# One attention, expert and gated-MLP kernel: routing weights transposed before they are normalised, and block outputs spread over steps

## The chip, the cores and the metric

The kernel runs as one program on one core of a Trainium2 chip. A core has a matrix engine (PE), a vector engine (DVE), a scalar engine (ACT), GpSimd (POOL) and a queue engine (SP) that issues most of the DMAs. Each engine works through its own instructions in order, and they meet through semaphores. The metric is the device time of one execution in microseconds; a kernel's time is the median over its runs. A profiled execution, whose time is given as well, has a trace of each instruction.

## The reference, cut to what matters

```python
def _attn_ref(q, k, v, p):                 # 4 batches, 8 heads, 576 tokens, head size 64
    p_packed = sm_attn(p, k, v)            # 32 packed queries
    return sm_attn(q, p_packed, p_packed)

def _moe_ref(x, domain_probs, w1, w2):     # x: 2304 x 512, E = 4 experts, F = 1024
    p = domain_probs / (domain_probs.sum(-1, keepdims=True) + 1e-09)
    for e in range(E):
        h = np.maximum(x @ w1[e], 0.0)
        out += p[:, e:e + 1] * (h @ w2[e])

def _moe2_ref(x, w_in, w_out, s, b):       # 512 -> 2048 -> 512
    r = np.maximum(x @ w_in, 0.0)
    return ((s * (r * r) + b) @ w_out).astype(np.float32)
```

The three run one after the other: attention, then a mixture of four experts in which every token goes through every expert with a weight p, then a gated MLP.

## The kernel before, in words

All large products are made of split operands, a high part (`hh`, `w2h`) and a remainder (`hl`, `w2l`), with three matmuls each.

**Steps of the expert stage.** The main loop runs over 256 steps, one for each (expert e, batch bi, half hf, block f of 128 hidden units). A part is the eight steps (f = 0 to 7) of one (e, bi, hf). In a step, `run(i)` first does what a table `weave` has for that step (attention work for the next batch, weight loads and splits, preparations of the last stage); `advance()` then calls `m1` for a unit two steps ahead, and `m2` works on the step's own unit. `m1` multiplies into a PSUM bank `h` (two of them) and evacuates it with a relu: ACT writes the high part, DVE the remainder. `m2` multiplies that into the accumulators `acc` (four banks, one for each block of 128 tokens). A batch of 576 tokens is four and a half blocks, so that in every second part `m1` leaves 64 columns over, which `rest` keeps, and which `m2` takes up in the part behind it. So 128 of the 256 `m1` calls evacuate two slices of one bank. At the last step of a part, `m2_out` takes each finished block (two or three of them) out of its bank on DVE, scaled by the block's weight from `p_tok`: L771 for e = 0, L774 otherwise, and for e = 3 a transpose L778 into `xt` behind it.

**Deferred work.** When three transposed blocks of a tile of `xt` are there, `x_turn` copies them on ACT into `x2` (L795), which the last stage reads. These copies, in eight pieces for each tile, lie in the list `later`; `go_on()` issues one piece of each list in it per step, behind `m2`.

**The weights p.** `probs` is loaded as 18 rows of 512 numbers (`p_rows`). At step 3 `expert_weights` sums, inverts and multiplies on DVE over 18 partitions (L1004 to L1008), PE transposes the product (L1014, four matmuls), and ACT copies it into `p_tok` (128 tokens x 72). The first use is at the end of the first part.

**What else stands there.** Ahead of the loop, PE has matmuls on zeros (`warm`, L979) in the gaps of the attention of batch 0. At step 3 batch 1's first scores `s` (L200) are computed from `kT`, which DVE transposes (L161). DVE has the maxima (L212) and ACT the copies (L214) of these scores, and the second half of the scores takes the same two banks. POOL makes `w2l` (L597) and parts of batch 0's last softmax (L348, L362). The last stage starts in the last ten steps: `m3` (L893) multiplies `xs` (L837, L838, from `x2`) with `wop`; a gate (L847, L850, L857, L861) gives `gg`, and `m4` (L929) multiplies that with `wo`.

The order within each engine is the order of the calls in the program; no scheduler moves anything.

## Time and profile before

| | |
|---|---|
| median of 3 runs | 1112.1 us (1112.06 to 1112.81) |
| the profiled execution | 1110.32 us |
| its span, first to last instruction | 1108.5 us |
| PE / DVE / ACT / POOL busy | 97% / 63% / 42% / 18% |
| PE idle, waits by line, the 15 largest groups | about 26 us in all, 7.0 of them at one place |
| mean granted clock of PE | 0.994 |

Busy shares say which engine the time goes through; where an engine that is 97% busy still waits, the list of waits gives the line, the engine that it waits for and how long. A granted clock of 1.00 is 2.4 GHz and 0.50 is 1.2 GHz. In a list of waits the columns are the waiting engine and line, the engine and line that ended the wait, and then the total, the number of waits and the longest. In a timeline they are start, duration, engine, line, operation, output and inputs with shapes, and in brackets the idle time before it and what ended it. Where neighbours are merged, x16 says how many a row holds.

### The profile page before, as it was taken

What the parts mean: (1) busy time and instruction counts of PE and PEld (TensorE: products, weight loads), DVE (VectorE), ACT (ScalarE), POOL (GpSimd) and SP (SyncE); (2) the same over time, 40 slices, a digit from 0 to 9 for tenths busy, and PEclk for the clock granted to TensorE, in tenths of its full rate; (3) what the DMA queues carried; (4) which work ended last, traced back from release to release, by engine and by line L of the source; (5) the groups of instructions that cost most, each with busy time, mean ns of one, the idle gap of its engine ahead of it and who ended that gap; (6) DMA issues with size and microseconds to landing.
All of it is one profiled execution on the core that took longest, in us unless ns stands there. A gap on an engine that the chain in (4) does not pass through costs nothing.

```text
span 1108.5 us, 16823 instructions
## 1 busy us (share of the span) xinstructions
PE 1078.5 (97%) x6248; PEld 918.5 (83%) x6248; DVE 694.3 (63%) x1309; ACT 467.7 (42%) x1023; POOL 198.4 (18%) x200
## 2 busy tenths in 40 slices
PE   8799999999999999999999999979999999999998
PEld 5577778878887788888887888869888988989987
DVE  7776665567576446556466644579845766675555
ACT  3433234454344344334435755686532332342121
POOL 1530303131200041001121122144211120210000
PEclk9899999999999999999999999999999999999999
DMA  9640411033116584674675341336756565555532
GB/s 269 194 108 25 104 49 39 10 102 117 57 61 240 194 228 136 202 233 146 220 195 156 102 124 57 124 142 247 281 203 211 181 219 177 210 199 184 196 114 86
DMA packets 66011, 170.21 MB, mean 154 GB/s; under 512 B 10489, under 2 KB 27129, under 8 KB 65931
## 3 DMA queue, kind: packets, MB, share of 16 engines
q1 hardware_dynamic: 65083, 168.03, 47.2%
q10 hardware_dynamic: 848, 1.11, 0.3%
q8 instruction: 50, 0.82, 0.3%
q14 instruction: 30, 0.25, 0.1%
HBM read 122.72 MB, written 46.40 MB: 153 GB/s over the span
## 4 chain that ended last, share of the span: by engine, by line
PE 83%; DVE 8%; ACT 5%; issue 2%; DMA 2%; SPq 1%; POOL 0%; ACTq 0%; DVEq 0%
PE acc L755 28%; PE o L929 18%; PE h L717 16%; PE h L893 15%; ACT x L795 1%; PE pp L518 1%; DVE hl L739 1%; PE s L318 1%; DVE xt L778 1%; DMA v<-in_v_dram 1%; ACT hh L738 1%; DVE acc L774 1%; PE pp L564 1%; PE s L200 1%; PE pv L266 1%
## 5 line engine op out<-in xcount | busy, mean ns | idle before, releaser
L717 PEld LDWEIGHTS h<-a,w1p 128*128 128x128 f32 x1536 | 226.3, 189 | 42.5 <-issue 13.5
L717 PE MATMUL h<-a,w1p 128*128 128x320 f32 (+1 forms) x1536 | 252.2, 299 | 7.5 <-DVE hl L739 4.5
L929 PE MATMUL o<-wo,gg 128*128 128x512 f32 x864 | 225.1, 394 | 2.2 <-DVE gg L861 2.2
L893 PE MATMUL h<-xs,wop 128*128 128x384 f32 x1008 | 206.2, 341 | 4.2 <-DVE xt L778 3.2
L755 PE MATMUL acc<-w2h,hh 128*128 128x512 f32 x512 | 201.9, 394 | 0.0
L755 PE MATMUL acc<-w2l,hh 128*128 128x512 f32 x512 | 201.7, 394 | 0.0
L755 PE MATMUL acc<-w2h,hl 128*128 128x512 f32 x512 | 200.2, 391 | 0.0
L893 PEld LDWEIGHTS h<-xs,wop 128*128 128x128 f32 x1008 | 183.4, 190 | 18.7 <-DVE xt L778 3.5
L739 DVE SCALAR_TENSOR_TENSOR hl<-h,hh 128x256 fp32r<-128x256 f32 x256 | 107.6, 420 | 142.3 <-ACT hh L738 141.7
L929 PEld LDWEIGHTS o<-wo,gg 128*128 128x128 f32 x864 | 160.7, 188 | 27.6 <-DVE gg L861 2.7
L738 ACT ACTIVATE hh<-h 128x256 fp32r<-128x256 f32 x256 | 97.0, 380 | 109.6 <-PE h L717 107.4
L755 PEld LDWEIGHTS acc<-w2h,hl 128*128 128x128 f32 x512 | 96.2, 188 | 22.1
L755 PEld LDWEIGHTS acc<-w2l,hh 128*128 128x128 f32 x512 | 96.4, 188 | 11.9
L755 PEld LDWEIGHTS acc<-w2h,hh 128*128 128x128 f32 x512 | 96.4, 188 | 10.8
L847 ACT ACTIVATE yy<-yy 128x768 f32<-128x768 f32 x48 | 40.3, 839 | 110.7 <-DVE yy L913 110.7
L913 DVE TENSOR_TENSOR yy<-h,uv 128x384 f32<-128x384 f32 x96 | 51.0, 551 | 48.5 <-PE h L893 48.3
L738 ACT ACTIVATE rest<-h 128x64 fp32r<-128x64 f32 x128 | 28.7, 225 | 89.9 <-DVE hl L739 89.9
L795 ACT ACTIVATE x<-xt 32x384 f32<-32x384 f32 x96 | 50.2, 523 | 20.5 <-DVE xt L778 18.9
L857 ACT ACTIVATE gg<-yy,b_sb 128x768 fp32r<-128x768 f32 x48 | 44.9, 935 | 32.0 <-DVE yy L850 31.7
L597 POOL TENSOR_TENSOR w2l<-w2r,w2h 128x512 fp32r<-128x512 f32 x24 | 31.1, 1297 | 129.0 <-ACT w2h L594 104.7
L861 DVE SCALAR_TENSOR_TENSOR gg<-yy,b_sb,gg 128x768 fp32r<-128x768 f32 x48 | 53.2, 1109 | 1.3 <-ACT gg L857 1.3
L739 DVE SCALAR_TENSOR_TENSOR rest<-h,rest 128x64 fp32r<-128x64 f32 x128 | 28.8, 225 | 37.2 <-ACT rest L738 37.2
(387 smaller groups left out, 1171.8 us busy)
## 6 DMA issues: line engine op xcount, KB each, us to landing
xs<-xs_dram SPq DMA_DIRECT2D x63, 768.0 KB, 4.3
w1p_dram<-w1o SPq DMA_DIRECT2D x32, 512.0 KB, 3.8
w1p<-w1p_dram SPq DMA_DIRECT2D x128, 128.0 KB, 4.4
xs_dram<-xs SPq DMA_DIRECT2D x21, 768.0 KB, 3.3
w1r<-in_moe_w_dram SPq DMA_DIRECT2D x12, 512.0 KB, 5.1
w2r<-in_moe_w_dram SPq DMA_DIRECT2D x24, 256.0 KB, 4.1
q<-in_q_dram SPq DMA_DIRECT2D x16, 288.0 KB, 7.0
out_dram<-o_sb SPq DMA_DIRECT2D x17, 256.0 KB, 2.1
```

Of the source, the lines that this page charges most:

```text
L597: nc.gpsimd.tensor_tensor(out=lo, in0=raw_t.pop((e, f)), in1=f32(hi), op=ALU.subtract)
L717: nc.tensor.matmul(t[:, : width(bi, hf)], lhsT=w1p_block(e, bi, f, gi, w), rhs=a2[bi][:, x, gi, part(bi, hf)], start=(n == 0), stop=(n == ...
L738: nc.scalar.activation(hi, src, AF.Relu)
L739: nc.vector.scalar_tensor_tensor(out=lo, in0=src, scalar=0.0, in1=f32(hi), op0=ALU.max, op1=ALU.subtract)
L755: nc.tensor.matmul(acc[j], lhsT=x, rhs=w, start=(f == 0 and n == 0), stop=(f == NF - 1 and n == 2),)
L795: nc.scalar.activation(dst[32 * q : 32 * q + 32, a], src[:, q], AF.Copy)
L847: nc.scalar.activation(y, y, AF.Relu)
L857: nc.scalar.activation(t[:, 0], y, AF.Identity, bias=b_sb)
L861: nc.vector.scalar_tensor_tensor(out=t[:, 1], in0=y, scalar=b_sb, in1=f32(t[:, 0]), op0=ALU.add, op1=ALU.subtract)
L893: nc.tensor.matmul(ps, lhsT=w[:, a, col], rhs=x[:, z, m, :], start=(n == 0), stop=(n == 3 * HK - 1),)
L913: nc.vector.tensor_tensor(out=dst, in0=ps, in1=src, op=ALU.add)
L929: nc.tensor.matmul(o_acc[i], lhsT=lhsT, rhs=w, start=(f == 0 and n == 0), stop=(f == FG - 1 and n == 2),)
```

## The change

Four things are edited. (1) `p_rows` is transposed as it is (`token_p`, four PE transposes and one ACT copy, called ahead of the loop behind the last `split_w2`, with nine warm matmuls behind it instead of ten), and `expert_weights`, still at step 3, then sums, inverts and multiplies `p_tok` in place, over 128 partitions: 18 sums of four numbers in each. PSUM tags in the prologue are renumbered. (2) `m1` issues both relus of a bank on ACT, and then both remainders on DVE. (3) At the end of a part `m2_out` is called for one block at once; the others go to `later`, one per step; the left-over block comes first instead of last, and the accumulators' numbering starts elsewhere. The last part's blocks all go to `later`. (4) `go_on()` stands ahead of `m2`, and a list of block copies starts with an entry that does nothing. In addition the raw weights of expert 0 have three tiles of their own in place of three slices of one.

```diff
+    *raw0, p_rows = (
+        keep.tile([P, NS, DM], F32, tag="x2", bufs=XB, name=f"raw0_{i}")[:, 0] for i in range(4)
+    )
...
         for (hi, lo), src in todo:
             nc.scalar.activation(hi, src, AF.Relu)
+        for (hi, lo), src in todo:
             nc.vector.scalar_tensor_tensor(
...
         if bi % 2 and not hf:
-            do.append((t0 - 1, rest.pop(f)))
+            do.insert(0, (t0 - 1, rest.pop(f)))
...
-            if f == NF - 1:
-                m2_out(e, j)
+        if f == NF - 1:
+            outs = [(m2_out, e, j) for j, _ in do]
+            if (e, bi, hf) != ua[-1][:3]:
+                m2_out(*outs.pop(0)[1:])
+            later.append(outs)
...
-                later.append([(x_turn, i, a, h) for a in range(4) for h in range(2)])
+                later.append(
+                    [(len, ())] + [(x_turn, i, a, h) for a in range(4) for h in range(2)]
+                )
...
-            dp = p_rows[:NB, 0].rearrange("j (a e) -> j a e", e=E)
-            ds = p_rows[:NB, 2, :P]
+            ds = att.tile([P, NB], F32, name="ds")
+            dp = p_tok.rearrange("a e j -> a j e")
             nc.vector.reduce_sum(ds, dp, axis=AX.X)
             nc.vector.tensor_scalar(ds, ds, 1e-9, None, ALU.add)
             nc.vector.reciprocal(ds, ds)
...
+                out=p_tok, in0=p_tok, in1=ds.unsqueeze(1).to_broadcast([P, E, NB]), op=ALU.mult
+            )
+
+        def token_p():
+            t = bank("p_tok", "h")[:, : E * NB].rearrange("a (e j) -> a e j", e=E)
+            rows = p_rows[:NB].rearrange("j (a e) -> j e a", e=E)
             for e in range(E):
-                nc.tensor.transpose(t[:, e, :], pn[:, e, :], ident[:NB, :NB])
+                nc.tensor.transpose(t[:, e, :], rows[:, e, :], ident[:NB, :NB])
             nc.scalar.activation(p_tok, t, AF.Copy)
...
-        keep_warm(10, "acc3")
+        token_p()
+        keep_warm(9, "acc0")
...
             advance()
+            if i < pos(0):
+                go_on()
             m2(*u)
-            if later and i < pos(0):
-                go_on()
...
+        while later and later[-1][0][0] is m2_out:
+            go_on()
```

PE at step 3, before: the transposes of p (`p_tok`) stand between the accumulation of step 2 and the scores `s` of batch 1.

```order
L755 MATMUL acc_544<-w2h_548,hl_537 128x512
L1014 MATMUL p_tok<-ident,p_rows 128x18 [waits DVE_49,PE_49]
L1014 MATMUL p_tok<-ident,p_rows 128x18 x3
L200 MATMUL s_100_636<-kT_555,pbd_520 64x288 [waits PE_49]
L200 MATMUL s_101_637<-kT_555,pbd_520 64x288 [waits Activation_49]
```

PE ahead of the loop, after: they stand behind batch 0's last scores and ahead of the warm matmuls.

```order
L318 MATMUL s_011_401<-qT_278,sbd_349 64x320
L1022 MATMUL p_tok<-ident,raw_3_94 128x18 [waits DMAHW5_49]
L1022 MATMUL p_tok<-ident,raw_3_94 128x18 x3
L986 MATMUL warm<-warm 128x512 [waits PE_49]
L986 MATMUL warm<-warm 128x512 x8
```

The wait on DVE is gone from these four, and at step 3 the scores follow the accumulation.

DVE at step 3, before: the four operations on p stand between the remainder `hl` and batch 0's last softmax (`at`, `r_011`), ahead of the maxima `m`.

```order
L739 SCALAR_TENSOR_TENSOR hl_606<-h_598,hh_605 128x256 [waits Activation_49]
L1004 TENSOR_REDUCE p_rows<-p_rows 18x128
L1005 TENSOR_SCALAR p_rows<-p_rows 18x128 [waits DVE_49]
L1006 RECIPROCAL p_rows<-p_rows 18x128 [waits DVE_49]
L1008 TENSOR_TENSOR p_rows<-p_rows 18x128x4 [waits DVE_49]
L371 STREAM_TRANSPOSE at_630<-sc_396 128x320 [waits Pool_49]
L359 TENSOR_REDUCE r_011_632<-sc_396 128x10
```

And after:

```order
L741 SCALAR_TENSOR_TENSOR hl_613<-h_605,hh_612 128x256 [waits Activation_49]
L1011 TENSOR_REDUCE ds<-p_tok 128x18
L1012 TENSOR_SCALAR ds<-ds 128x18 [waits DVE_49]
L1013 RECIPROCAL ds<-ds 128x18 [waits DVE_49]
L1014 TENSOR_TENSOR p_tok<-p_tok,ds 128x72 [waits DVE_49]
L371 STREAM_TRANSPOSE at_632<-sc_398 128x320 [waits Pool_49]
L359 TENSOR_REDUCE r_011_634<-sc_398 128x10
```

They keep their place, with fewer elements for each partition.

DVE at the end of a part of the last expert (`acc` with `p_tok` is the sum, the transpose into `xt` follows it; `wop` and `xs` belong to the last stage), before:

```order
L739 SCALAR_TENSOR_TENSOR hl_7678<-h_7670,hh_7677 128x256 [waits DVE_49,Activation_49]
L774 SCALAR_TENSOR_TENSOR acc_7481<-acc_7481,p_tok,xt_2306 128x512 [waits PE_49]
L778 STREAM_TRANSPOSE xt_2306<-acc_7481 128x512 [waits DVE_49]
L774 SCALAR_TENSOR_TENSOR acc_7485<-acc_7485,p_tok,xt_2534 128x512 [waits PE_49]
L778 STREAM_TRANSPOSE xt_2534<-acc_7485 128x512 [waits DVE_49]
L774 SCALAR_TENSOR_TENSOR acc_7489<-acc_7489,p_tok,xt_2306 128x512 [waits PE_49]
L778 STREAM_TRANSPOSE xt_2306<-acc_7489 128x512 [waits DVE_49]
L695 TENSOR_TENSOR wop_7709<-wi_7316,wop_7709 128x256 [waits DMAHW4_49,DMAHW3_49,Activation_49]
```

And after:

```order
L779 SCALAR_TENSOR_TENSOR acc_7484<-acc_7484,p_tok,xt_2330 128x512 [waits PE_49]
L783 STREAM_TRANSPOSE xt_2330<-acc_7484 128x512 [waits DVE_49]
L696 TENSOR_TENSOR wop_7704<-wi_7318,wop_7704 128x256 [waits DMAHW4_49,DMAHW3_49,Activation_49]
L696 TENSOR_TENSOR wop_7704<-wi_7340,wop_7704 128x256 [waits Activation_49]
L845 TENSOR_TENSOR xs_7709<-s_0_7180,xs_7709 128x768 [waits DMAHW3_49,Activation_49]
L741 SCALAR_TENSOR_TENSOR hl_7721<-h_7713,hh_7720 128x256 [waits Activation_49]
L920 TENSOR_TENSOR yy_7662<-h_7732,uv_7663 128x384
L779 SCALAR_TENSOR_TENSOR acc_7488<-acc_7488,p_tok,xt_2597 128x512
L783 STREAM_TRANSPOSE xt_2597<-acc_7488 128x512 [waits DVE_49]
```

The third block now stands one step further back, behind the next remainder.

ACT and DVE in a step with a left-over slice, before (`hh` and `rest` on ACT with the waits of each, then `hl` and `rest` on DVE):

```order
L738 ACTIVATE hh_3142<-h_3135 128x256 [waits PE_49,Activation_49]
L738 ACTIVATE rest_3144<-h_3135 128x64 [waits DVE_49]
...
L739 SCALAR_TENSOR_TENSOR hl_3143<-h_3135,hh_3142 128x256 [waits Activation_49]
L739 SCALAR_TENSOR_TENSOR rest_3144<-h_3135,rest_3144 128x64 [waits Activation_49]
```

And after:

```order
L739 ACTIVATE hh_3144<-h_3137 128x256 [waits PE_49,Activation_49]
L739 ACTIVATE rest_3146<-h_3137 128x64
...
L741 SCALAR_TENSOR_TENSOR hl_3145<-h_3137,hh_3144 128x256 [waits PE_49,Activation_49]
L741 SCALAR_TENSOR_TENSOR rest_3146<-h_3137,rest_3146 128x64
```

ACT's second relu has lost its wait for DVE; DVE's `hl` now waits for the count that ACT reaches with the second relu.

PE at the start of the last stage, behind the last accumulation (`h` from `xs` and `wop` are six matmuls of a unit each), before:

```order
L755 MATMUL acc_7733<-w2h_6243,hl_7891 128x512
L893 MATMUL h_7947<-xs_7714,wop_7709 128x384 [waits DVE_49]
L893 MATMUL h_7947<-xs_7714,wop_7709 128x384 x5
L893 MATMUL h_7968<-xs_7781,wop_7774 128x384 x6
L893 MATMUL h_7984<-xs_7781,wop_7774 128x384 [waits DVE_49]
```

And after:

```order
L757 MATMUL acc_7728<-w2h_6244,hl_7889 128x512
L900 MATMUL h_7941<-xs_7709,wop_7704 128x384 [waits DVE_49]
L900 MATMUL h_7941<-xs_7709,wop_7704 128x384 x5
L900 MATMUL h_7967<-xs_7779,wop_7772 128x384 x6
L900 MATMUL h_7981<-xs_7779,wop_7772 128x384 x6
L900 MATMUL h_7995<-xs_7842,wop_7837 128x384 x6
L900 MATMUL h_8013<-xs_7842,wop_7837 128x384 [waits DVE_49]
```

The wait for DVE that stood ahead of the third unit stands ahead of the fifth.

## Rows read from the trace of the kernel before

**Rows 1.** the page's first part: engine, busy time and share of the span, instructions

```profile
PE 1078.5 (97%) x6248; PEld 918.5 (83%) x6248; DVE 694.3 (63%) x1309; ACT 467.7 (42%) x1023; POOL 198.4 (18%) x200
```

**Rows 2.** PE's waits, longest in total first: us, times, longest

```profile
PE p_tok L1014 <- DVE p_rows L1008: 7.0, 1, 7.0
PE h L717 <- DVE hl L739: 4.5, 5, 1.7
PE h L893 <- DVE xt L778: 3.2, 1, 3.2
PE o L929 <- DVE gg L861: 2.2, 1, 2.2
...
PE h L717 <- DVE rest L739: 1.8, 3, 0.9
...
PE h L717 <- POOL a L382: 1.1, 1, 1.1
PE acc L755 <- DVE xt L778: 1.0, 2, 0.8
```

**Rows 3.** relus and remainders of the left-over slices: busy, mean ns, idle before

```profile
L738 ACT ACTIVATE rest<-h 128x64 fp32r<-128x64 f32 x128 | 28.7, 225 | 89.9 <-DVE hl L739 89.9
...
L739 DVE SCALAR_TENSOR_TENSOR rest<-h,rest 128x64 fp32r<-128x64 f32 x128 | 28.8, 225 | 37.2 <-ACT rest L738 37.2
```

**Rows 4.** timeline of PE behind step 2: start, duration, instruction

```profile
35.25 0.39 PE L755 MATMUL acc<-w2h,hl 128*128 128x512 f32 x1
```

**Rows 5.** timeline of PE, the scores at steps 3 and 4

```profile
43.15 2.58 PE L200 MATMUL s<-kT,pbd 64*64 64x288 f32 x16
...
48.29 1.20 PE L200 MATMUL s<-kT,pbd 64*64 64x288 f32 x16
```

**Rows 6.** timeline of DVE at step 3

```profile
36.29 2.28 DVE L161 STREAM_TRANSPOSE kT<-k 128x576 f32<-128x576 f32 x2
...
38.75 0.65 DVE L1004 TENSOR_REDUCE p_rows<-p_rows 18x128 f32<-18x512 f32 x1
39.43 1.03 DVE L1005 TENSOR_SCALAR p_rows<-p_rows 18x128 f32<-18x128 f32 x1
...
41.47 1.02 DVE L1008 TENSOR_TENSOR p_rows<-p_rows 18x512 f32<-18x512 f32 x1
...
42.76 0.44 DVE L359 TENSOR_REDUCE r<-sc 128x10 f32<-128x330 f32 x1
43.24 0.22 DVE L360 RECIPROCAL r<-r 128x10 f32<-128x10 f32 x1
```

**Rows 7.** stretches at step 3 and in the last stage: busy, PEclk, DMA

```profile
42.60:46.40 3.80, 3.77 (x23) 2.47 (x24) 1.45 (x5) 0.37 (x2) 0.73 (x1) 0.50 0.88 324
731.70:735.90 4.20, 4.20 (x15) 4.20 (x16) 1.93 (x4) 4.08 (x8) 1.28 (x1) 0.59 0.02 4
746.10:749.50 3.40, 3.40 (x10) 3.11 (x11) 2.76 (x4) 3.34 (x6) 0.00 (x0) 0.51 0.06 23
```

**Rows 8.** timeline of PE at the start of the last stage

```profile
731.68 2.58 PE L893 MATMUL h<-xs,wop 128*128 128x384 f32 x9 [3.15 <-DVE xt L778]
```

**Rows 9.** timeline of POOL at step 3

```profile
39.12 1.26 POOL L597 TENSOR_TENSOR w2l<-raw,w2h 128x512 fp32r<-128x512 f32 x1
```

**Rows 10.** timeline of ACT at 80 us

```profile
80.23 0.22 ACT L738 ACTIVATE rest<-h 128x64 fp32r<-128x64 f32 x1 [2.39 <-DVE hl L739]
80.35 0.73 ACT L381 ACTIVATE a<-at 128x640 fp32r<-128x640 f32 x1
```

**Rows 11.** timeline of DVE at the end of a part of expert 0

```profile
235.39 1.40 DVE L771 TENSOR_SCALAR xt<-acc,p_tok 128x512 f32<-128x512 f32 x2
236.71 0.67 DVE L574 TENSOR_TENSOR w1p<-pp,w1p 64x512 fp32r<-64x512 f32 x1
```

**Rows 12.** timeline of ACT at a block copy

```profile
624.62 1.06 ACT L795 ACTIVATE x<-xt 32x384 f32<-32x384 f32 x2 [4.76 <-DVE xt L778]
```

**Rows 13.** timeline of DVE at the start of the last stage

```profile
731.55 0.98 DVE L913 TENSOR_TENSOR yy<-h,uv 128x384 f32<-128x384 f32 x2
```

More of the change, by code (lines that the diff above doesn't have):

```diff
@@ L576, in attention_experts_mlp_kernel @@
     raw_t = {}
-    raw0 = keep.tile([P, NS, DM], F32, tag="x2", bufs=XB, name="raw0")
-    p_rows = keep.tile([P, NS, DM], F32, tag="x2", bufs=XB, name="p_rows")
+    *raw0, p_rows = (
+        keep.tile([P, NS, DM], F32, tag="x2", bufs=XB, name=f"raw0_{i}")[:, 0] for i in range(4)
+    )
     def load_w2(e, f):
@@ L584, in load_w2 @@
         else:
-            raw = raw0[:, f % NS]
+            raw = raw0[f % 3]
         nc.sync.dma_start(out=raw, in_=w2[e, f * P : (f + 1) * P, :])
@@ L752, in m2 @@
                 n = acc["n"] = (acc.get("n", -1) + 1) % KB
-                acc[j] = ps_acc.tile([P, DM], F32, tag=f"acc{n}", name=f"acc_{e}{j}")
+                acc[j] = ps_acc.tile([P, DM], F32, tag=f"acc{(n + 3) % KB}", name=f"acc_{e}{j}")
             for n, (x, w) in enumerate(((xh, wl), (xh, wh), (xl, wh))):
@@ L963, in attention_experts_mlp_kernel @@
         nc.sync.dma_start(
-            out=p_rows[:NB, 0], in_=probs.rearrange("(j a) e -> j (a e)", a=P)
+            out=p_rows[:NB], in_=probs.rearrange("(j a) e -> j (a e)", a=P)
         )
@@ L1006, in expert_weights @@
             nc.vector.reciprocal(ds, ds)
-            pn = p_rows[:NB, 1].rearrange("j (e a) -> j e a", e=E)
             nc.vector.tensor_tensor(
-                out=pn.rearrange("j e a -> j a e"), in0=dp,
-                in1=ds.unsqueeze(2).to_broadcast([NB, P, E]), op=ALU.mult,
-            )
-            t = bank("p_tok")[:, : E * NB].rearrange("a (e j) -> a e j", e=E)
+                out=p_tok, in0=p_tok, in1=ds.unsqueeze(1).to_broadcast([P, E, NB]), op=ALU.mult
+            )
+        def token_p():
+            t = bank("p_tok", "h")[:, : E * NB].rearrange("a (e j) -> a e j", e=E)
+            rows = p_rows[:NB].rearrange("j (a e) -> j e a", e=E)
             for e in range(E):
-                nc.tensor.transpose(t[:, e, :], pn[:, e, :], ident[:NB, :NB])
+                nc.tensor.transpose(t[:, e, :], rows[:, e, :], ident[:NB, :NB])
             nc.scalar.activation(p_tok, t, AF.Copy)
@@ L1041, in attention_experts_mlp_kernel @@
         keep_warm(3, "h")
-        at_s2(0, 0, ("acc0", "acc1"))
+        at_s2(0, 0, ("acc1", "acc2"))
         for gi in range(G):
-            at_pt(0, gi, f"acc{2 + gi}")
+            at_pt(0, gi, f"acc{3 - 3 * gi}")
         fold_w1(0, 0)
-        at_s2(0, 1, ("acc0", "acc1"))
+        at_s2(0, 1, ("acc1", "acc2"))
         for gi in range(G):
```

## The prediction

> **What bounds the kernel now.** I read the engines' busy shares first, then PE's waits, and then the timeline around each wait. PE is busy for 1078.5 us of the 1108.5 us span, 97% [rows 1], so that only what PE waits for, or does at a lower clock, can be won. The change takes no matmul out of the loop. The list of waits names the places [rows 2]: 7.0 us once, for the normalised p at step 3; 4.5 us in five waits of `m1` for a remainder on DVE; 3.2 and 2.2 us once each at the start of the last stage; 1.8 us in three waits for the remainder of a left-over slice; 1.1 us behind a POOL operation; 1.0 us in two accumulators that aren't read out yet. They sum to 20.8 us, and the change touches the code in front of every one of them. The ceiling is thus about 21 us and what the clock gives back. The other engines matter only where they release PE late: the 89.9 us that ACT's second relu waits for DVE, and the 37.2 us the other way round [rows 3], lie beside PE's matmuls except in those few places.
>
> **The stall at step 3.** PE's last matmul of step 2 starts at 35.25 and takes 0.39 us [rows 4]; the next thing is p's transposes, 7.0 us later, and the scores behind them start at 43.15 [rows 5]. DVE is what PE waits for: it transposes `kT` from 36.29 for 2.28 us, then comes a remainder, and then the four operations on p from 38.75 to 41.47 + 1.02 = 42.49 [rows 6]. With p's transposes ahead of the loop, the scores need `kT`, which is there at 36.29 + 2.28 = 38.57. They start 43.15 - 38.57 = 4.6 us earlier, and a stall of 38.57 - 35.64 = 2.9 us is left: the next late thing is a transpose of `kT`, not nothing.
>
> Then the clock. Behind the 7.0 us stall PE runs at 0.50 up to 46.40 [rows 7], and sixteen scores take 2.58 us where the same sixteen take 1.20 us later [rows 5]. From 43.15 to 46.40 at half speed costs 3.25 / 2 = 1.6 us, which goes with that stall. But the stall of 2.9 us that is left may bring the clock down as well. The trace has two stalls of about that size: 3.15 us [rows 8] with a stretch at 0.59 behind it, and 2.2 us [rows 2] with 3.4 us at 0.51 behind it [rows 7]. Either costs (1 - 0.51) x 3.4 or (1 - 0.59) x 4.2, thus 1.7 us. As both were followed by it, I take 1.7 us as given back.
>
> The new operations on p are not free. They stay at the same place on DVE with 18, 18, 18 and 72 elements for a partition instead of 512, 128, 128 and 512. Nearest from below are the reduce of 330 elements to 10, 0.44 us, and a reciprocal of ten, 0.22 us [rows 6]: four times 0.18 would be 0.7 us. Nearest from above is the addition of 1e-9 itself: 1.03 us for 128 elements [rows 6], which is long for its size; it starts at 39.43 while POOL's subtraction runs from 39.12 to 40.38, and ends 0.08 us behind that [rows 9]. So 1.7 us is the other end. The second half of the scores takes the banks of the first, which DVE and ACT have to empty behind these operations; by 0.7 us nothing should be late, by 1.7 us that 1.0 us shows. I take 1.0 us, since the row is the same operation at the same place. Ahead of the loop, four small transposes stand for one warm matmul there; between nothing (PE fills time) and 0.3 us, I take 0.1 us. **Sum for step 3: 4.6 + 1.6 - 1.7 - 1.0 - 0.1 = 3.4 us**, between 2.9 and 6.2.
>
> The Trainium skill, page "SBUF — State Buffer", section "Who interferes with whom", has a rule that speaks against this place: a DVE instruction with two SBUF inputs, or one like `tensor_scalar` in its two-port mode, and a GpSimd instruction that reads SBUF shut each other out for the whole of the instruction. By it the addition and the multiplication wait for POOL's subtraction whatever their size, and the sum is as above; without it the time would be 1.0 us shorter. The 1.03 us that ended with POOL's instruction agrees.
>
> **The two remainders of a bank.** Before, ACT and DVE take turns on a bank with a left-over slice: relu, remainder, relu, remainder. After, ACT does both relus without a wait, and DVE both remainders behind them. Each of the 128 `hl` comes later by ACT's second relu, 225 ns, and the last read of the bank comes earlier, as one exchange between the engines falls away (ACT's 89.9 us / 128 = 0.7 us of waiting for DVE [rows 3] is what that exchange takes on average, in which DVE mostly does something else). What PE gets: at 80 us, ACT's second relu waits 2.39 us for DVE, and the copy that POOL and then PE need stands behind it [rows 10]; without the wait all 1.1 us of the POOL row [rows 2] go. Of the three waits for a left-over remainder, 1.8 us, I take 1.2 us, as in one of them DVE itself is late with other work. The bounds are 0.3 us of the first and 0.5 us of the second, and all 2.9 us.
>
> **One block at a time.** At an end of a part of expert 0, two read-outs, 1.40 us, stand in front of a subtraction that the next fold waits for [rows 11]; PE's longest wait for a remainder, 1.7 us, follows. With one moved a step back, 0.7 us of it go. For the last expert a block takes a sum and a transpose, and with the left-over block first, its bank is read out first: the two waits for an accumulator, 1.0 us [rows 2], go but for 0.1 us. What stands behind the moved read-outs one and two steps later is the next remainder; a block of 0.7 to 1.4 us fits into a step's idle time on DVE (37% of the span [rows 1]), so I charge nothing, and up to 0.5 us at each of some four places for the range.
>
> **Block copies.** A copy that waits for the last transpose holds the relu behind it: at 624.62 ACT starts two copies of 1.06 us after 4.76 us of waiting, and the relu `hh` stands behind them [rows 12]. A step or more later the transpose is long done. This happens at two tiles. The four waits for a remainder other than the one of 1.7 us share 2.8 us [rows 2], and two of them stand here: an even share is 1.4 us, two copies of 1.06 us would be 2.1, and I take 1.7. The other two, 1.1 us then, have other copies or `xs` in front, of which I take 0.5 us. Together 2.2 us, between 1.0 and 2.8.
>
> **The start of the last stage.** PE waits 3.15 us until 731.68 [rows 8] for the last transpose, behind two units. After, it waits behind four. Nine matmuls took 2.58 us there with the clock partly at half [rows 8], so the twelve of two units take 1.7 us at full clock and 3.4 at half; I take 2.1, as most of the stretch ahead of the stall is at full clock. But the last transposes have two sums of `yy` ahead of them now that stood behind them, 0.98 us [rows 13]. 2.1 - 1.0 = 1.1 us come off. The gate wait of 2.2 us [rows 2] a little later sits behind ACT's copies, which come earlier or later by some tenths; I take 0.7 us of it. Sum 1.8 us; the bounds are a loss of 0.5 us (that wait grows) and 5 us (both go, and with them one stretch at half clock).
>
> The raw tiles give the DMAs other places, but no DMA is in front of PE at these steps; nothing.
>
> **Sum.** 3.4 + 1.1 + 1.2 + 0.7 + 0.9 + 2.2 + 1.8 = 11.3 us. The profiled execution, 1110.3 us, would come to 1099.0; its span lies 1.8 us below its time, which nothing here touches. The median is 1112.1, and 1112.1 - 11.3 = **1100.8 us**.
>
> **Rivals.** *The clock stays up* behind the 2.9 us stall: 1.7 us better, 1099.1. For it speaks that the stall is shorter than 3.15 us, against it that 2.2 us was enough. *Only step 3 is won*: PE's small waits move to the next late thing on DVE or ACT, which are as busy as before: 1112.1 - 3.4 = 1108.7. For it: every other gain is below 2.3 us, and DVE does the same work. Against: several of these waits are a short operation behind a long one, which a change of order does resolve. *Nearly every listed wait goes*, with the clock in both places: 1112.1 - 20.8 = 1091.3. *Slower:* PE comes to wait for `hl`. It is 225 ns later in 128 steps; if PE stood behind it each time, 28.7 us [rows 3] would be added, 1129.5; the turning point is 11.3 / 0.225 = 50 of the 128 steps. Against it: the list has five waits for `hl` in all 256 steps, so that `hl` is ahead of PE by more than that nearly everywhere. *The change doesn't do what it says*: the transposes ahead of the loop hold PE for p's load, or the waits fall on other instructions of the same chain; 1112.
>
> **How the numbers follow.** Forecast 0.48, clock stays up 0.22, only step 3 0.13, nearly all 0.10, slower 0.04, nothing 0.03. The range from 1091 to 1109 holds the first four, each with some width, and leaves out the last two and edges. Two measurements of this kernel can be told apart by about 0.2%, 2.2 us; faster 0.93, same 0.03, slower 0.04 in that sense.
>
> **What would show it.** In the profile after, the 7.0 us row is replaced by a wait of the scores for `kT` of about 2.9 us; a stretch behind it is at 0.5 or it is not; the addition takes 0.2 us or ends with POOL's subtraction; the POOL row and the accumulator rows are gone; ACT's `rest` has no idle time with DVE's name; the waits for `hl` fall to about 2 us; the last stage's wait is about 2 us and stands one pair of units later. A wait for `hl` in dozens of steps would prove me wrong, as would a stall at step 3 that keeps its length under another name.

## The result

| | before | changed |
|---|---|---|
| median | 1112.08 us (1110.61 to 1112.81) | 1095.05 us (1093.99 to 1095.63) |
| span of the profiled execution | 1108.5 us | 1092.0 us |

The ratio is 0.9847, with a 95% interval from 0.9830 to 0.9864: 17.0 us less. I had forecast 1100.8 us, 11.3 us less, in a range from 1091 to 1109. So the direction and the range were right, and the gain was half as large again as the sum.

Where it came from is seen by cutting both traces at four events on PE: the first `m1` matmul, the first of the second half of batch 1's scores (step 4), the last accumulation of the expert stage, and the end of PE's last matmul. Each entry is the time from the event before:

| kernel | first `m1` at | to the second scores | to the last accumulation | to the end of PE |
|---|---|---|---|---|
| before | 26.29 | 22.00 | 677.76 | 378.57 |
| changed | 26.73 | 17.09 | 668.95 | 375.43 |
| gain | -0.4 | 4.9 | 8.8 | 3.1 |
| as forecast | -0.1 | 3.5 | 6.1 | 1.8 |

The three gains were all larger than forecast, and none had the wrong sign; the loss ahead of the first `m1` is within what that start varies by from one profiled execution to the next (last section).

### The profile page after: what moved, and what is told of

Same layout as the page of the kernel before. It is cut to its first block, busy times and chain, and to the rows that moved or that the text cites. A ratio compares the mean times of both kernels' runs of the same rounds, so it can differ in the third digit from the quotient of the medians.

```text
span 1092.0 us, 16889 instructions
## 1 busy us (share of the span) xinstructions
PE 1073.5 (98%) x6247; PEld 915.9 (84%) x6247; DVE 677.6 (62%) x1309; ACT 456.6 (42%) x1023; POOL 198.5 (18%) x200
## 4 chain that ended last, share of the span: by engine, by line
PE 91%; ACT 3%; DVE 3%; issue 1%; DMA 1%; SPq 0%; ACTq 0%; DVEq 0%
PE acc L757 34%; PE h L718 18%; PE o L936 18%; PE h L900 15%; PE pp L518 1%; PE s L318 1%; DMA v<-in_v_dram 1%; PE s L200 1%; PE pw L416 1%; ACT x L802 1%; PE pv L266 1%; PE pp L564 1%; DVE w1p L574 0%; ACT w2h L595 0%; ACT hh L739 0%
## 5 line engine op out<-in xcount | busy, mean ns | idle before, releaser
L741 DVE SCALAR_TENSOR_TENSOR hl<-h,hh 128x256 fp32r<-128x256 f32 x256 | 107.8, 421 | 183.6 <-ACT rest L739 100.3
L900 PE MATMUL h<-xs,wop 128*128 128x384 f32 x1008 | 203.8, 338 | 3.1 <-DVE xt L783 2.0
L900 PEld LDWEIGHTS h<-xs,wop 128*128 128x128 f32 x1008 | 181.0, 188 | 17.5 <-DVE xt L783 2.3
L920 DVE TENSOR_TENSOR uv<-h,uv 128x384 f32<-128x384 f32 x48 | 26.4, 554 | 39.7 <-PE h L900 39.7
L857 DVE SCALAR_TENSOR_TENSOR yy<-yy,s_sb 128x768 f32<-128x768 f32 x48 | 50.8, 1058 | 0.0
```

What stands on the lines that cost most here:

```text
L741: nc.vector.scalar_tensor_tensor(out=lo, in0=src, scalar=0.0, in1=f32(hi), op0=ALU.max, op1=ALU.subtract)
L857: nc.vector.scalar_tensor_tensor(out=y, in0=y, scalar=s_sb, in1=y, op0=ALU.mult, op1=ALU.mult)
L900: nc.tensor.matmul(ps, lhsT=w[:, a, col], rhs=x[:, z, m, :], start=(n == 0), stop=(n == 3 * HK - 1),)
L920: nc.vector.tensor_tensor(out=dst, in0=ps, in1=src, op=ALU.add)
```

## The profile after

PE's waits after, in the same form as [rows 2] (waiting engine and line, what ended the wait, us in total, number, longest):

```profile
PE o L936 <- DVE gg L868: 3.0, 2, 2.2
PE s L200 <- DVE kT L161: 2.4, 1, 2.4
PE h L900 <- DVE xt L783: 2.0, 1, 2.0
...
PE h L718 <- DVE hl L741: 1.5, 2, 1.0
...
PE h L900 <- DVE xs L845: 0.8, 1, 0.8
```

Against [rows 2]: the 7.0 us for p is gone, and a wait of 2.4 us for `kT` has taken its place. The POOL row, the accumulator row and the row of the left-over remainders aren't there any more. Five waits for `hl`, 4.5 us, have become two with 1.5 us. The wait for the last transpose is 2.0 us where it was 3.2 (L900 is the L893 of before), and the one for the gate has kept its 2.2 us, with a second one of 0.8 us beside it.

The groups of instructions that answer to [rows 3] (busy, mean ns of one, idle before it, and what ended most of that):

```profile
L741 DVE SCALAR_TENSOR_TENSOR hl<-h,hh 128x256 fp32r<-128x256 f32 x256 | 107.8, 421 | 183.6 <-ACT rest L739 100.3 <-ACT hh L739 81.3
...
L739 ACT ACTIVATE rest<-h 128x64 fp32r<-128x64 f32 x128 | 27.9, 218 | 0.0
L741 DVE SCALAR_TENSOR_TENSOR rest<-h,rest 128x64 fp32r<-128x64 f32 x128 | 27.3, 213 | 0.0
```

The 89.9 us and 37.2 us that ACT and DVE waited for each other over the left-over slices are 0.0 and 0.0. What remains is `hl` waiting for ACT's second relu, 100.3 us in all, nearly all of it beside PE's matmuls.

Step 3 on PE:

```profile
35.77 0.70 PE L200 MATMUL s<-kT,pbd 64*64 64x288 f32 x4
38.82 2.15 PE L200 MATMUL s<-kT,pbd 64*64 64x288 f32 x12 [2.35 <-DVE kT L161]
...
43.82 1.20 PE L200 MATMUL s<-kT,pbd 64*64 64x288 f32 x16
```

The four scores that need the first half of `kT` run at once, from 35.77; the other twelve wait 2.35 us. These twelve take 2.15 us, where all sixteen of the second half take 1.20 us: PE is at half clock again, as the stretch behind the wait shows (PE, PEld, DVE, ACT, POOL busy, granted clock, DMA):

```profile
38.90:42.30 3.40, 3.40 (x18) 2.08 (x19) 3.26 (x10) 0.13 (x1) 2.18 (x3) 0.50 0.73 174
```

DVE at that place, and POOL:

```profile
39.23 0.27 DVE L1012 TENSOR_SCALAR ds<-ds 128x18 f32<-128x18 f32 x1
...
39.83 0.94 DVE L1014 TENSOR_TENSOR p_tok<-p_tok,ds 128x72 f32<-128x72 f32 x1
```

```profile
39.43 1.26 POOL L598 TENSOR_TENSOR w2l<-raw,w2h 128x512 fp32r<-128x512 f32 x1
```

The addition takes 0.27 us, and the sum and the reciprocal are as short. The multiplication of 72 elements takes 0.94 us: it starts at 39.83, and ends at 40.77, 0.08 us behind POOL's subtraction (39.43 + 1.26 = 40.69).

## Experiments

All ratios are to the kernel before, measured on the same chip, with 95% intervals; "us" are medians, and a gain in us beside a ratio is taken from the ratio. The kernels of this section ran on two chips, on which the kernel before took 1112.0 to 1112.2 and 1110.7 us (the second for the kernel without the empty entry, the doubled relu and the two first ones with matmuls on zeros), so that kernels of different chips are better compared by their ratios.

### Each part alone

The first three kernels are the kernel before with one part of the change; the fourth is the changed kernel with one part taken back.

**p alone.** `token_p()` ahead of nine warm matmuls, `expert_weights` on `p_tok`.

```diff
-            dp = p_rows[:NB, 0].rearrange("j (a e) -> j a e", e=E)
-            ds = p_rows[:NB, 2, :P]
+            ds = att.tile([P, NB], F32, name="ds")
+            dp = p_tok.rearrange("a e j -> a j e")
...
-        keep_warm(10, "acc3")
+        token_p()
+        keep_warm(9, "acc3")
```

> The kernel before with one part of the change: p transposed raw ahead of the loop, normalised by tokens at step 3; everything else as before. Theory A (the parts each remove their own waits and add up): step 3 is worth what the aligned traces of before and after show there, 4.5 to 5.0 us less than before, so about 1107.3 us; the second half of the scores behind the stall is not late, and the clock still falls to one half for one stretch behind a stall of 2.4 to 2.9 us. Theory B (the step 3 sum of the prediction, with 1.0 us for the wait for POOL): 3.4 us less, about 1108.7. Theory C (step 3 only shortens because the other edits made room): 0 to 2 us less.

Measured: 1106.46 us, ratio 0.9955 (0.9942 to 0.9969), 5.0 us less. To the second scores 17.06 us instead of 22.00, and from there to the last accumulation 677.72 against 677.76: the part works at its one place and nowhere else. The waits that the other edits are about have the size that they had before, as two of them show beside the new one for `kT`:

```profile
PE h L717 <- DVE hl L739: 4.5, 5, 1.7
...
PE s L200 <- DVE kT L161: 3.0, 2, 2.4
...
PE h L717 <- DVE rest L739: 1.7, 3, 0.9
```

Theory A, and not the 3.4 us of my sum.

**Order of relus and remainders alone.**

```diff
         for (hi, lo), src in todo:
             nc.scalar.activation(hi, src, AF.Relu)
+        for (hi, lo), src in todo:
             nc.vector.scalar_tensor_tensor(
```

> The kernel before with one part of the change: both relus of a bank first, then both remainders. Theory A (it resolves single places): the wait behind POOL at 80 us goes (1.3 us), the two at 582 and 585 us shrink by 0.3 to 0.5 us each, the one at 688 us by 0.4 us; 2.0 to 3.0 us less than before, about 1109.5 us. Rival (the second remainder's lead is paid by the first one's delay of 0.225 us): new waits for hl in more than five steps, time the same or up to 28.7 us more.

Measured: 1106.39 us, ratio 0.9956 (0.9942 to 0.9970), 4.9 us less, twice what I had expected. From the second scores to the last accumulation it is 671.86 us, 5.9 less than before. The waits show why:

```profile
PE p_tok L1015 <- DVE p_rows L1009: 6.5, 1, 6.5
PE h L717 <- DVE hl L740: 4.5, 5, 1.7
```

The rows for POOL and for the left-over remainders are gone, which I had counted in part, and so is the row for the accumulators, 1.0 us in [rows 2], which I had given to the read-outs alone: my reading, which no run separates, is that the read-outs stand behind DVE's second remainder, which no longer waits for ACT. There are five waits for `hl` with 4.5 us, as before: its delay of 0.225 us costs nothing that this list shows.

**Read-outs one per step alone.**

```diff
-            if f == NF - 1:
-                m2_out(e, j)
+        if f == NF - 1:
+            outs = [(m2_out, e, j) for j, _ in do]
+            if (e, bi, hf) != ua[-1][:3]:
+                m2_out(*outs.pop(0)[1:])
+            later.append(outs)
...
+            if i < pos(0):
+                go_on()
             m2(*u)
-            if later and i < pos(0):
-                go_on()
```

> The kernel before with one part of the change: one block read out at the end of a part and the others one per step, the left-over block first, the deferred work called ahead of m2, the last part's blocks deferred; the list of copies has no empty entry. Theory A: the wait at 237.5 us loses 0.7, the two for accumulators 1.5 with what the pipeline loses behind a wait, the two behind block copies 2.1 (the copies already come a step after the last transpose), the start of the last stage 3.1; 7 to 8 us less than before, about 1104.5 us. Theory B (the block copies need the empty entry): the waits at 625 and 643 us stay, 5 to 6 us less, about 1106.5 us.

Measured: 1108.18 us, ratio 0.9963 (0.9953 to 0.9973), 4.1 us less; the largest expectation of the three gave the smallest gain. Between the second scores and the last accumulation 5.1 us are won. But from there to the end it takes 379.57 us, 1.0 more than before, although the wait for the last transpose shrank:

```profile
PE h L896 <- ACT xs L840: 2.2, 1, 2.2
PE h L896 <- DVE xt L781: 2.0, 1, 2.0
...
PE h L717 <- DVE hl L739: 1.6, 2, 1.1
```

3.2 us of waiting for the transpose have become 2.0, and a new wait of 2.2 us for ACT's `xs` has come. About half of the 1.0 us lies behind the first `o`, where PE is at half clock for 10.2 us on end in this execution. The two waits behind block copies are gone without the empty entry, so Theory B falls, and the entry must be there for something else.

**Everything but the order of relus and remainders.** The diff of the second kernel, taken back in the changed kernel.

> The changed kernel with the order of relus and remainders as before. Theory A (parts add up): 2 to 3 us more than the changed kernel, about 1097.5 us, the POOL wait at about 76 us is back with 1.1 us. Rival (with the blocks read out one per step the exchange of the two engines no longer holds anyone up but at 76 us): 1.3 us more, about 1096.4 us.

Measured: 1100.27 us, ratio 0.9901 (0.9881 to 0.9920), 4.1 and 5.2 us more than the two measurements of the changed kernel. POOL's 1.1 us and one accumulator wait are back:

```profile
PE h L718 <- DVE hl L740: 1.5, 2, 1.0
...
PE h L718 <- POOL a L382: 1.1, 1, 1.1
...
PE acc L756 <- DVE xt L782: 0.7, 1, 0.7
```

The three parts alone sum to 5.0 + 4.9 + 4.1 = 14.0 us of the 17.0 (by the medians 15.5). In the middle stretch the last two overlap (5.9 + 5.1 against 8.8): either removes the three waits for a left-over remainder, 1.8 us in [rows 2]. The accumulator waits are not among what both remove. With the read-outs alone 0.7 us of them is left, as it is here, and only the order of relus and remainders takes them away. In the last stage something is still missing, the fourth part.

### The empty entry

```diff
-                later.append(
-                    [(len, ())] + [(x_turn, i, a, h) for a in range(4) for h in range(2)]
-                )
+                later.append([(x_turn, i, a, h) for a in range(4) for h in range(2)])
```

> The changed kernel without the empty entry at the head of a list of block copies, so that each copy comes one step earlier. Theory A (the copies are behind the last transpose anyway, as the blocks are read out one per step): nothing changes at the places of 625 and 643 us, and the start of the last stage keeps its gain, 1095.0 us. Theory B (the empty entry matters at the start of the last stage, where the part with blocks read out one per step alone showed a wait of 2.2 us for ACT's xs): up to the last accumulation nothing changes, from there to the end 2 to 3 us more, 1097.5 us.

Measured: 1098.66 us, ratio 0.9892 (0.9877 to 0.9907). From the last accumulation to the end 378.44 us, where the changed kernel takes 375.43 and the kernel before 378.57. So the gain at the start of the last stage goes with this one entry (Theory B). What it does is seen on ACT, in the timeline of this kernel and then of the changed one (start, duration, operation, and in brackets the idle time before):

```profile
714.76 1.05 ACT L800 ACTIVATE x<-xt 32x384 f32<-32x384 f32 x2
720.62 1.06 ACT L800 ACTIVATE x<-xt 32x384 f32<-32x384 f32 x2 [4.80 <-DVE xt L783]
721.71 0.63 ACT L706 ACTIVATE wo<-wo 128x512 fp32r<-128x512 f32 x1
722.24 0.83 ACT L842 ACTIVATE xs<-x 128x768 fp32r<-128x768 f32 x1
```

```profile
715.64 0.63 ACT L706 ACTIVATE wo<-wo 128x512 fp32r<-128x512 f32 x1
716.18 0.83 ACT L844 ACTIVATE xs<-x 128x768 fp32r<-128x768 f32 x1
719.35 1.06 ACT L802 ACTIVATE x<-xt 32x384 f32<-32x384 f32 x2 [2.35 <-DVE xt L783]
```

Without the entry, the next copies, which wait for the last transpose, stand in front of ACT's `wo` and `xs`: ACT waits 4.80 us and then does those two. With it, both are done before the wait, which is 2.35 us. And behind the wait ACT has no time to make up for it, as the stretches show (PE, PEld, DVE, ACT, POOL busy, granted clock, DMA), for the changed kernel:

```profile
724.00:727.00 3.00, 1.91 (x10) 1.27 (x9) 1.95 (x3) 2.94 (x6) 1.75 (x2) 1.00 0.00 0
727.00:730.00 3.00, 0.95 (x5) 0.51 (x3) 3.00 (x2) 2.95 (x6) 1.38 (x1) 1.00 0.65 262
```

ACT is busy for 2.94 and 2.95 of 3 us, PE for 1.91 and 0.95. DVE is as full as ACT in the second stretch, 3.00 of 3 us, so these rows alone don't name the bound; the sizes do. In the kernel before, ACT waited 4.95 us in front of such a copy:

```profile
731.72 2.12 ACT L795 ACTIVATE x<-xt 32x384 f32<-32x384 f32 x4 [4.95 <-DVE xt L778]
```

From the last accumulation to the first `o` (PE's first matmul of `m4`) the kernel before takes 17.18 us and the changed one 14.56: 2.62 less, where ACT's idle time became 4.95 - 2.35 = 2.60 less. The kernel without the entry takes 17.00, 2.44 more, where ACT's idle time is 4.80 - 2.35 = 2.45 more.

The other 0.5 of the 3.1 us is not the entry's. Behind the first `o` the changed kernel takes 360.87 us, and the kernel before 361.39. But the second profile of the changed kernel ("changed kernel again" below) takes 361.51 there. In it PE is once at half clock,

```profile
732.80:736.20 3.40, 3.40 (x11) 2.60 (x10) 3.37 (x5) 3.30 (x6) 0.00 (x0) 0.51 0.48 201
```

as PE is twice in the kernel before [rows 7]; in the first profile of the changed kernel the clock stays up through the last stage until 1090 us. So the entry is worth 2.4 to 2.6 us, and the rest varies between executions.

If ACT's idle time is the price, the remaining 2.35 us should be there to win:

```diff
-                    [(len, ())] + [(x_turn, i, a, h) for a in range(4) for h in range(2)]
+                    [(len, ())] * (3 if i == NT3 - 1 else 1) + [(x_turn, i, a, h) for a in range(4) for h in range(2)]
```

> The changed kernel with three empty entries instead of one at the head of the last tile's list of copies. Theory A (at the start of the last stage ACT is what sets the time, and its idle time in front of a copy that waits for the last transposes, 4.8 us without an empty entry and 2.35 us with one, goes through to the end): the copy comes two units later, ACT does other work first, and 1 to 2.3 us less from the last accumulation to the end, 1093.5 us. Rival (PE's wait of 2.0 us for the last transpose sets the time there): nothing more to win, 1095.0 us.

Measured: 1096.92 us, ratio 0.9863 (0.9847 to 0.9879); the changed kernel beside it 1096.13. From the last accumulation to the first `o` it takes 13.39 us, 1.2 less than the 14.59 there, as Theory A has it. But ACT's idle time did not get less, it moved: the copies no longer wait, and `yy` in their place does.

```profile
720.95 0.85 ACT L854 ACTIVATE yy<-yy 128x768 f32<-128x768 f32 x1 [2.73 <-DVE yy L920]
```

And behind the first `o` more is lost than was won: ACT's copies now stand further back, in front of what empties an output bank,

```profile
PE o L936 <- DVE gg L868: 2.9, 2, 2.2
...
PE o L936 <- ACT o_sb L948: 1.9, 1, 1.9
```

a wait that the changed kernel does not have, and behind it PE is at half clock from 742.8 to 746.2. From the last accumulation to the end it is 377.95 us, 1.9 more than the changed kernel beside it (376.10). The kernel with the later blocks at expert 0's end, below, has the same last stage; in its profile PE is at half clock earlier (6.8 us from 729.4), waits only 0.10 us for that copy, and takes 376.40 us. So neither theory holds to the end: the copy's wait was worth 1.2 us up to the first `o`, and what it costs behind that changes with the clock.

### The stall that is left at step 3

```diff
+                if (bi, h, e, g) == (1, 0, 0, 1):
+                    keep_warm(9, "acc1")
```

> The changed kernel with nine matmuls on zeros between the first four scores of step 3 and the twelve that wait for kT, in a bank that nothing uses there: PE does idle work where it had waited 2.35 us. Theory A (the stall that is left brings the clock down, which costs half of the slow stretch): the granted clock stays at 1.00 there, the twelve scores and the m1 behind them take 1.6 us less together; of that the second half of the scores gives back up to 0.7 us, because its banks are empty only at 42.9 us, held up on DVE by the multiplication that ended with POOL's subtraction. 1093.5 to 1094.2 us. Rival (the clock falls whatever PE does there, or the slow stretch is hidden behind DVE): the same time as the changed kernel, 1095.0 us.

Measured: 1096.16 us, ratio 0.9874 (0.9859 to 0.9889). The clock stayed up, and the twelve scores take 1.19 us instead of 2.15:

```profile
40.98 2.35 PE L988 MATMUL warm<-warm 128*128 128x512 f32 x9
43.41 1.19 PE L202 MATMUL s<-kT,pbd 64*64 64x288 f32 x12
```

```profile
43.40:45.40 2.00, 1.99 (x19) 1.36 (x20) 1.90 (x7) 0.00 (x0) 0.75 (x1) 1.00 0.60 149
```

To the second scores it is 15.65 us instead of 17.09: 1.4 us, near Theory A's 1.6. The time of the kernel doesn't show them. Its next stretch is 670.38 us against 668.95, 1.4 longer, and the wait that has grown is that for the exponentials at step 5 (L239, which is the L237 of the others), 1.04 us in one place where the changed kernel has 0.44. The exponentials need `nm`, which DVE makes of the maxima. In the changed kernel, and then in this one with POOL beside it:

```profile
45.81 0.34 DVE L221 SCALAR_TENSOR_TENSOR nm<-m,nscale 128x1 f32<-128x1 f32 x2
```

```profile
48.95 0.98 DVE L223 SCALAR_TENSOR_TENSOR nm<-m,nscale 128x1 f32<-128x1 f32 x2
49.03 0.89 POOL L384 TENSOR_TENSOR a<-at,a 128x320 fp32r<-128x320 f32 x1
```

Two operations on one element a partition take 0.64 us longer, and end at 49.93, 0.01 us behind POOL's subtraction (49.92): scores that come earlier bring `nm` into that subtraction. That is 0.6 of the 1.4 us. Another 0.6 us is lost at 582 us, behind a wait of 0.41 us for `rest` that neither profile of the changed kernel has; why it comes is left open. With p normalised at step 5 instead of 3,

```diff
-                at(3, expert_weights)
+                at(5, expert_weights)
```

> As the one before, and in addition the normalising of p on DVE two steps later (step 5 instead of 3). Theory A: the maxima of the first half of the scores come 1.7 us earlier on DVE, the second half finds its banks empty, and the whole 1.6 us of the clock are won: 1093.4 us. Rival (the operations on p were not what held the second scores): the same as without the shift, and new waits of PE at step 5 or 6 for a remainder behind the shifted operations.

it was 1095.58 us, ratio 0.9866 (0.9850 to 0.9883): 15.52 us to the second scores, and 670.29 us behind them. So the operations on p were not what held that place up, and the rival holds. `nm` did: it takes 1.05 us in this kernel (44.65 to 45.70), beside a subtraction of POOL that ends at 45.55, and the wait for the exponentials is 1.15 us. All together, with one more edit at the end of expert 0 tried first by itself,

```diff
-            if (e, bi, hf) != ua[-1][:3]:
+            if (e, bi, hf) not in (ua[-1][:3], (0, B - 1, 1)):
```

> As the one before, and both blocks of expert 0's last part are read out later, none at once. Theory A (the read-out in front of the subtraction that the next fold waits for is what is left of the wait at 232 us): that wait falls from 1.0 to about 0.4 us, 0.6 us less, 1092.9 us. Rival (the read-out then stands in front of the next remainder): the same time, a wait of PE for hl about 3 us later.

> All together: three empty entries, both blocks of expert 0's last part later, nine matmuls on zeros in the wait for kT and p normalised at step 5. Theory A (each is worth what its own stretch showed): up to the second scores 1.5 us less than the changed kernel, of which a longer wait for the exponentials at step 5 takes 0.7 us back; 0.6 us at expert 0's end, 1 to 2.3 us at the last stage: 1092.2 us. Rival (the kept clock is given back in full): 1092.9 us or more.

> The changed kernel once more, beside the next three on one chip, so that differences of one or two microseconds can be read. 1095.0 us as before, within 1 us; its ratio to the kernel before 0.985.

| kernel | median | ratio, interval |
|---|---|---|
| changed kernel again | 1096.13 us | 0.9859 (0.9841 to 0.9877) |
| three empty entries, blocks later at expert 0's end | 1096.41 us | 0.9860 (0.9845 to 0.9874) |
| all together | 1095.15 us | 0.9846 (0.9831 to 0.9861) |

At expert 0's end the two waits for `hl` went from 1.5 to 1.0 us as expected, with no new wait behind them in the list:

```profile
PE h L718 <- DVE hl L741: 1.0, 2, 0.5
```

None of the three differs from the changed kernel by more than the intervals. The times expected for the last kernels, 1092.2 to 1093.5 us, were all missed, and the changed kernel itself came out 1.1 us above its first measurement, where I had allowed 1. That the small gains are real can be read from the stretches, that they sum to a faster kernel can't be said.

### How much room `hl` has

```diff
         for (hi, lo), src in todo:
             nc.scalar.activation(hi, src, AF.Relu)
+        for (hi, lo), src in todo[1:]:
+            nc.scalar.activation(hi, src, AF.Relu)
```

> The changed kernel with ACT's relu of the left-over slice done twice in each of the 128 steps that have one, so that DVE's first remainder waits another 0.225 us. It computes the same. Theory A (the remainder is ahead of PE nearly everywhere, so the delay that the order brings costs nothing): within 1 us of the changed kernel, 1095.0 to 1096.0 us, waits for hl in no more than a handful of steps. Rival (the remainder is only just in time): up to 28.7 us more, and waits for hl in tens of steps.

Measured: 1097.34 us, ratio 0.9880 (0.9865 to 0.9895), 1.2 and 2.3 us more than the two measurements of the changed kernel, and by the ratios (0.9859 and 0.9847) 2.3 and 3.7 us more.

```profile
PE h L718 <- DVE hl L743: 1.6, 2, 1.0
...
PE h L718 <- DVE rest L743: 0.7, 1, 0.7
PE acc L759 <- DVE xt L785: 0.7, 1, 0.7
```

A further 0.225 us in 128 steps is 28.8 us if PE stood behind it; it brought two new waits of 0.7 us, and none for `hl`. So the slower rival was far from its turning point: not 50 steps but two are near the edge, and one of these two, at 579 us, is the place where the kernel with the matmuls on zeros waits 0.41 us for `rest` without a doubled relu. By them I missed the 1 us of my expectation.

## Why the prediction was right, and where its sum was off

**Step 3: the path was right, two of its sizes were not.** The scores start behind `kT` and the clock falls behind the stall that is left; both are in the trace after. The stall is 2.35 us and not 2.9, as four of the scores need only the first half of `kT`, which I had not looked at: 0.5 us. The other 1.0 us is the term for DVE's operations, held up by POOL. DVE was held (0.94 us for the multiplication), but PE, at half clock, came to the second scores when their banks were empty. ACT's copies out of them end at 42.17 + 0.77 = 42.94, and the scores start at 43.82 without a wait:

```profile
42.17 0.77 ACT L214 ACTIVATE a<-s 128x288 f32<-128x288 f32 x2 [3.44 <-DVE m L212]
```

Where PE's clock stayed up behind the same stall, a part of the term can show: in the kernel without the empty entry the second scores waited 0.41 us for ACT's copy out of those banks, and took 1.56 us instead of 1.20.

```profile
40.16 1.19 PE L200 MATMUL s<-kT,pbd 64*64 64x288 f32 x12 [2.36 <-DVE kT L161]
...
44.03 1.56 PE L200 MATMUL s<-kT,pbd 64*64 64x288 f32 x16 [0.41 <-ACT a L214]
```

With the doubled relu, where the clock stayed up as well, that wait was 0.08 us, and with the matmuls on zeros there was none. So I had added the slow clock and a delay that the slow clock hides, and had made the delay too large for either clock. The lower bound of 0.7 us for the four operations had no row for its 0.18 us each; where POOL doesn't hold them they take 0.17 to 0.27 us each. The Trainium skill's rule ("SBUF — State Buffer", "Who interferes with whom") agrees with the rows of DVE and POOL as far as the hold goes; the rule tells the length of the hold, and not whether anybody waits for it.

**The two remainders: right in kind, too small.** 1.1 us at 80 us were 1.3 by the start of the matmuls; of the left-over waits I took 1.2 of 1.8 us and all went. The mis-sized term is the list of waits itself: it counts idle time of PE, and a wait costs about 0.16 us more than that. The longest wait of [rows 2] for a remainder shows it: the last accumulation in front of it starts at 237.50 and the next `m1` at 239.58. Of these 2.08 us 1.68 are in the list; the accumulation itself lasts 0.40 us, of which 0.23 is all that it takes when the next matmul follows at once, and the other 0.17 is lost. Nine such waits went, 6.9 us in the list (3.0 for `hl`, 1.8, 1.1 and 1.0), which adds about 1.5 us to the middle stretch, of the 2.7 us by which I had it too small; another 0.6 us is the part of the left-over waits that I had left standing.

**One block at a time: half right, and half by luck.** Of the 0.7 us at 237.5 us 0.65 went; the wait there is 1.03 us long now. The accumulators' waits, of which I had taken 0.9 us for the left-over block that comes first, went too, but not by that: with the read-outs alone 0.7 us of them stays. The order of relus and remainders takes them away.

**Block copies: right in size, for the wrong part.** The waits at 625 and 643 us went, 1.8 us in the list and 2.1 us with what each costs behind it; but the read-outs one per step do that, not the empty entry, whose delay of a step I had counted on.

**The start of the last stage: the step that failed.** I priced it by PE's two waits, and added what is behind ACT as "some tenths". The price that fits is ACT's idle time in front of the copy, 4.95 us before and 2.35 after: 2.60 us, of which PE's first `o` shows 2.62. Behind that wait the changed kernel's ACT has no idle time over 0.15 us until 742 us. PE's gate wait, of which I took 0.7 us, didn't change at all (2.2 us), and still the stretch became 3.1 us shorter, 0.5 of them by PE's clock in that execution. I had the row with an ACT wait for a transposed block in front of me [rows 12], and used it only for the middle.

**The slower rival and the doubtful ones** are settled by the runs: `hl` has room; the small waits did not just move on; the clock did fall. In the middle stretch the terms came out low for one reason: I took shares of waits, where the change removed most of them whole, and each with what it costs beyond its idle time.

## What to carry to other kernels

When two engines take turns on one bank, they can be made to work one behind the other, by writing all of the first engine's operations ahead of the second's. Look for it where the first engine's second operation has idle time with the second engine's name, and take the gain from the few places where PE waits (here 4.9 us), not from that idle time (89.9 us). Doubling the delay that the new order brings shows how much room there is.

Where another engine than PE has no gap for a long stretch, price a change there by that engine's idle time ahead of the stretch, whatever PE's waits say; put work that can't be late in front of a wait in its queue, and look at what the moved work then stands in front of.

A stall, the slow clock behind it and what is late next are not a sum. Work out what is late next for either clock.

## What I had not expected of the hardware

**The same stall does or doesn't bring the clock down.** Eight profiled executions have the stall of 2.35 us in front of the twelve scores. In six of them the granted clock went to 0.50 behind it, in two it stayed at 1.00. The stretch behind the stall in the changed kernel run again, and in the kernel with the doubled relu:

```profile
40.00:42.00 2.00, 2.00 (x13) 0.70 (x6) 1.90 (x5) 0.00 (x0) 1.34 (x2) 0.50 0.99 210
```

```profile
40.00:42.00 2.00, 2.00 (x20) 1.38 (x13) 1.90 (x7) 0.25 (x1) 2.00 (x3) 1.00 0.63 168
```

In the three executions with matmuls on zeros in the stall it stayed up every time. The Trainium skill, page "TensorE: Matmul & The Clock Gate", section "Why this matters for your kernels", advises against idle gaps between bursts of matmuls, as the clock goes back behind them. It has longer gaps in mind than this one; six of the eight show that 2.35 us can be enough, and two that it need not be. Up to the second scores the six take 16.93 to 17.09 us and the two 15.64 and 15.97, so that the slow clock cost 1.0 to 1.5 us there when it came. The times of the kernels with matmuls on zeros do not show it.

**Which instruction ends with POOL's changes from run to run.** In the changed kernel's second profile it was the addition of 18 elements, and the multiplication was quick:

```profile
40.13 1.24 DVE L1012 TENSOR_SCALAR ds<-ds 128x18 f32<-128x18 f32 x1
...
41.70 0.23 DVE L1014 TENSOR_TENSOR p_tok<-p_tok,ds 128x72 f32<-128x72 f32 x1
```

```profile
40.08 1.26 POOL L598 TENSOR_TENSOR w2l<-raw,w2h 128x512 fp32r<-128x512 f32 x1
```

40.13 + 1.24 = 41.37, and POOL's subtraction ends at 40.08 + 1.26 = 41.34. The same addition took between 0.17 and 1.25 us in these runs, for 18 elements a partition, and `nm` between 0.34 and 1.05 us for two operations on one element. Which of them falls into a subtraction of POOL decides whether PE sees it: the addition and the multiplication cost PE from nothing to 0.8 us (0.41 in front of the second scores and 0.36 within them, in the kernel without the empty entry), `nm` costs it what it is held for (0.34 us of `nm` go with a wait of 0.44 us for the exponentials, 0.52 with 0.61, 0.98 with 1.04 to 1.06).

**The start varies more than the edits.** The first `m1` matmul starts between 26.3 and 28.3 us in most of the profiled executions, and at 31.2 us in one (the kernel with the warm matmuls only), in which PE waited 1.7 us for the loaded `v`; where it starts before 27 us that wait is 0.4 us or isn't there. A kernel's times scatter by about as much, which fits though no run here separates the two, and differences of 1 us between the last kernels could be read from stretches of the trace only.
